# The backward pass of a gated S4 layer: two token tiles in turns at the opening of the last pass, a block of the gated gradient kept on chip, and a write on another queue

## The chip, the cores and the metric

The kernel runs on one core of a Trainium2 chip. The core has five engines, each with its own instruction stream: TensorE (PE in the profile, its weight loads PEld), VectorE (DVE), ScalarE (ACT), GpSimd (POOL) and SyncE (SP). DMAs are issued by SP, ACT and POOL. The metric is the device time of one execution in microseconds (us); the median over the runs is compared.

## The reference

The forward pass is a layer norm, an S4 convolution over the sequence, a SwiGLU feed-forward network whose output goes through a SiLU, and a gated sum. The program computes the output and the gradients of all inputs (B_x is not differentiated).

```python
x = A_u                                  # 1 x 2048 x 576
xn = _layernorm(x, axis=-1)
s = _A_ref(xn, A_re, A_im, B_re, B_im, C_re, C_im, log_dt, Dskip)
                                         # long convolution by FFT, 128 states
g = _silu(_B_ref(xn, w1, w3, w2))        # out = (silu(x w1) * (x w3)) w2, F = 4608
return x + s * g
...
_out, _vjp = jax.vjp(_f, A_u, A_A_re, ..., B_w1, B_w3, B_w2)
return (_out0, *_vjp(grad_out))
```

## The kernel before

Everything is in bf16 on the matmul side with f32 sums. The sequence of 2048 tokens is cut into 16 token tiles of 128 (LT), the width 576 (D) into two matmul pieces of 288, and the hidden width 4608 (F) into 36 blocks of 128 (FT) and 18 groups of 256. In the odd token tiles the 128 tokens stand in reversed order. The last pass takes the token tiles in the order 1, 3, .. 15, 0, 2, .. 14. "Tile i" of the last pass is the i-th of that order. Results of the odd ones go to a scratch array first (`odd`) and are written from there to the output with the tokens turned back.

The order of instructions on each engine is made by a scheduler from the program's order, from due times (`self.at`) and from `issue_after`, which puts an instruction behind another one. Buffers come from pools; a tile with the tag of another takes its slot, and a tile that takes a slot waits until the old one is read for the last time.

The stages, in the order in which they run:

1. Layer norm, convolution kernel and forward convolution beside the first half of the network (`ffn_hidden`).
2. `ffn_output`: for each of the 16 token tiles the product with w2 (`po`, L975), and then its epilogue. It works out `gs_t`, the gradient times the gate (L994), and stores it to `GS_dram` (L995) in four quarters of 144 columns.
3. `backward` opens. `ssm_bwd_conv` is a generator: `conv_bwd_quarter` for quarter 0 loads `gs` in four blocks of four token tiles (L1114), folds each (L1130, L1131), transforms it (`dft_folded`, L740), multiplies spectra on DVE (`Z`, L777 to L786, `ZZ`, L1161 and L1166) and transforms back (L751). Between its steps it yields to `phase6_group`, which for group 0 makes all its gradient tiles: `make(s)` is a product of the transposed gradient with w2 (`ph`, L1552), an ACT copy (L1555) and DVE products (L1568). The order written is: conv blocks 0 to 2, then `make` 0 to 2 and the last transposes, then conv block 3, then the rest.
4. The groups of the feed-forward backward, gi = 0 to 17. Each forms `gg_n` and `gu_n` (gradients of gate and up), stores them to `GG_dram` and `GU_dram` (L1573), and forms the weight gradients: `phase6_grad13` for w1 and w3 (L1610, L1620, L1622), and `phase6_grad2` for w2 (`pgw`, L1590). The w2 gradient of a group is made inside the same group, at its stages h1 and h3, except for groups 16 and 17: theirs come after the stores of group 17. From group 11 on, half steps of the S4 parameters are mixed in (`param_half`: PE L1224, DVE L1229 and L1232; loads `qT` and `gz` on SP, `pz` on ACT), and `phase5_blocks` turns their sums into the S4 gradients (POOL DMAs L1286, L1317, L1328). From there on all DMAs of SP keep the order in which they are written (`self.chain`).
5. The last pass, `phase6_inputs`. For each tile i there are 72 steps of two matmuls (L1657, 128 x 288): a block of `GG` or `GU` in transposed form (`acts`, loaded by a transposing DMA) against a row block of w1 or w3, also transposed (`wA`, `wT`). The 72 row blocks lie in pieces; `load_piece` loads one as five transposes into a slot that the groups have done with. Then come the layer norm's backward (`ln_bwd_tile`, L1668 to L1696, on DVE, ACT and POOL) and `ln_finish` (L1699), which writes the result (ACT queue, L1703) and at i = 5 and i = 9 one half of the reversed odd tiles (SP, L1706). There are two `acts` buffers, so that those of tile i + 2 can only be loaded when tile i has been multiplied. Parameter half steps stand at fixed steps of a tile (`stops`).

Where the last pass opens, SP's order is: `acts` of tile 0; ten transposes (`h_n` 1,22 and `h_n` 0,22); the GG half of tile 1; ten transposes (`gg_n` 0,29 and `gu_n` 1,29); the GU half of tile 1; `qT`, `gz`, `qT`, `gz`; `acts` of tile 2, and so on.

Of the kernel before, what the change touches and what calls it, by code (L numbers as in the profile page):

```python
# [14 lines left out]
BF16 = mybir.dt.bfloat16  # L15
I32 = mybir.dt.int32
I16 = mybir.dt.int16
P = 128
# [58 lines left out]
class K:  # L77
# [849 lines left out]
    def ffn_output(self, T0, TB):  # L927
# [9 lines left out]
        with self.pool(name="o_hc", bufs=1) as hpc, \  # L937
# [10 lines left out]
            self.epi = []  # L948
            w2 = []
# [29 lines left out]
            def finish(st):  # L979
# [16 lines left out]
                                  in_=gs_t[:].rearrange("p (g d) -> p g d", g=4))  # L996
                nc.vector.tensor_tensor(out=n4(g[:]), in0=p4(s_t[:]), in1=n4(g[:]), op=ALU.mult)
# [102 lines left out]
    def conv_bwd_quarter(self, g, kp, zp, ps, T0, TQ):  # L1100
# [9 lines left out]
        for b in range(NB if g == 0 else 1):  # L1110
            ts = slice(b * KT, (b + 1) * KT) if g == 0 else slice(0, LT)
            if g == 0:
                self.at(T0 - 170 + 40 * b if b < NB - 1 else T0)
            nc.sync.dma_start(out=gs[:, ts], in_=self.GS_dram[g, :, ts])  # L1114
# [9 lines left out]
        G = []  # L1124
        gm = kp.tile([P, NB, 2, W], BF16, name="gm")
        g4 = gs[:].rearrange("p (b k) w -> p b k w", k=KT)

        def fold(bs):
            lo, hi = g4[:, bs, 0:2], g4[:, bs, 3:1:-1]
            nc.vector.tensor_tensor(out=gm[:, bs], in0=lo, in1=hi, op=ALU.subtract)  # L1130
            nc.vector.tensor_tensor(out=lo, in0=lo, in1=hi, op=ALU.add)  # L1131
# [4 lines left out]
        for b in range(NB):  # L1136
            self.at(T0 + (TQ * 0.05 * b if g else 0))
            after = None
            if g == 0 and b == NB - 1:
                pt = ps.tile([P, 512], FP32, name="et_ps")  # L1140
                self.turn_go(LT - 1, pt[:].bitcast(BF16)[:, 0:cfg.DT * P].rearrange("p (c t) -> p c t", t=P), self.dft_last)
                yield
                self.at(T0)
                after = self.pe_last
            G.append(self.bgp.tile([P, 1, 2, KT, W], BF16, name=f"g_{b}"))
            if g == 0:
                fold(slice(b, b + 1))
            with self.tc.issue_after(after.ins) if after is not None else nullcontext():
                self.dft_folded(ps, self.cCS, (g4[:, b], gm[:, b]), G[b])
            if after is not None:  # L1150
                yield
# [192 lines left out]
    def backward(self, T0, TG, TQ, TC, TX, gctx, mats):  # L1344
# [12 lines left out]
        with ExitStack() as out:  # L1357
# [18 lines left out]
            conv = self.ssm_bwd_conv(T0, TQ, ps)  # L1376
            next(conv)
# [4 lines left out]
            group = self.phase6_group(0, cur, elp, gwp, ps_h, ps_gw)  # L1382
            next(group)
# [14 lines left out]
            for gi in range(NG):  # L1398
# [9 lines left out]
                for stage in group if gi == 0 else self.phase6_group(gi, cur, elp, gwp, ps_h, ps_gw):  # L1408
# [4 lines left out]
                    if stage in ("h1", "h3"):  # L1413
                        if gi < NG - 2:
                            w2(gi, stage == "h3")
                        if stage == "h3" and gi + 2 < NG:
                            self.phase6_load_h(gi + 2, T0 + TG * gi, inp)
                    if stage == "h1" and lastg:
                        self.load_piece(wT, inp, "gg_n", 0, 15, 7)
                        self.load_piece(wT, inp, "gu_n", 1, 15, 7)  # L1420
                        self.load_piece(wT, wp, "w2T", 1, 13, 2)
# [3 lines left out]
                    if stage == "stored":  # L1425
# [3 lines left out]
                        if lastg:  # L1429
# [3 lines left out]
                            for g in (NG - 2, NG - 1):  # L1433
                                for fl in range(2):
                                    w2(g, fl)
                                step()
                                self.phase5_step(self.half // 2)
                                self.phase5_step(self.half // 2)
                                if g == NG - 2:
                                    self.load_piece(wT, inp, "h_n", 1, 22, 7)  # L1440
                                else:
                                    self.load_piece(wT, inp, "h_n", 0, 22, 7)
                            acts.append(self.load_acts(1, (0,)))
# [11 lines left out]
            self.load_acts(1, (1,), acts[1])  # L1455
# [77 lines left out]
    def phase6_group(self, gi, tiles, elp, gwp, ps_h, ps_gw):  # L1533
# [24 lines left out]
        if gi == 0:  # L1558
            for s in range(3):
                make(s)  # L1560
            yield "early"
# [74 lines left out]
    def phase6_inputs(self, T2, TX, wT, acts, pool):  # L1636
# [6 lines left out]
        with pool(name="l_sb", bufs=2) as sb, pool(name="l_s1", bufs=1) as s1, \  # L1643
                pool(name="l_sm", bufs=4) as sm, pool(name="x_ps", bufs=2, space=bass.MemoryType.PSUM) as ps:
            for i in range(LT):
                self.at(T2 + TX * i)
                act, t = acts[i], self.order[i]
# [4 lines left out]
                go_t, o1 = go_o1[:, 0], go_o1[:, 1]  # L1652
                nc.scalar.dma_start(out=go_t, in_=self.tok("grad_out", t))
                stops = () if i in (0, LT - 1) else (14, 38, 62) if i in (2, 4, 6, 8) else (20, 50)
                for n, (ai, fi, w) in enumerate(steps):
                    for pi_, (po, pw) in enumerate(pieces):
                        self.pe_last = nc.tensor.matmul(px[pi_][:, 0:pw], lhsT=act[:, ai, fi, :], rhs=w[:, po:po + pw],  # L1657
                                                        start=(n == 0), stop=(n == len(steps) - 1))
                    if n == 8 and i > 0:
                        self.ln_finish()  # L1660
                    if i == LT - 1 and n in (20, 32, 44, 64):
                        self.phase5_step(self.half // 2)
                    if n in stops:
                        self.param_step()
                        self.phase5_step(self.half // 2)
                gx = s1.tile([P, D], FP32, name="gx7")
# [32 lines left out]
    def ln_finish(self):  # L1699
# [4 lines left out]
        if i in (5, 9):  # L1704
            q = slice(0, 4) if i == 5 else slice(4, 8)
            self.nc.sync.dma_start(out=self.turned(self.aps["out_1"].flatten_outer_dims(), q.start, q.stop), in_=self.odd["out_1"][q])  # L1706
# [99 lines left out]
```

## Time and profile before

| | |
|---|---|
| three runs, median | 1875.47 us (1872.55 to 1878.48) |
| the profiled execution, its own time | 1874.95 us |
| its span in the profile | 1873.2 us |
| mean granted TensorE clock over the span | 0.973 |
| PE busy | 1689.1 us, 90% of the span |
| PE weight loads busy | 1231.2 us, 66% |
| DVE busy | 1370.1 us, 73% |
| ACT busy | 910.0 us, 49% |
| POOL busy | 352.1 us, 19% |
| DMA | 417.27 MB, mean 223 GB/s |
| L1657, matmuls with wT | x1408, 182.5 us; 17.3 us idle before them, by wT |
| L1657, matmuls with wA | x896, 123.4 us; 19.6 us idle before them, 19.1 by acts |
| L1590 (w2 gradient) | x1152, 150.4 us |
| L1552 (gradient to the hidden width) | x1440, 173.0 us |

A busy engine is not one at its peak, and idle time counts only on the engine that ends last in that stage. So the page is read stage by stage: in a table of windows each line has its start and end, its length, then busy us (and number of instructions) of PE, PEld, DVE, ACT and POOL, PE's granted clock as a share of full speed, the busy share of the DMA engines, and GB/s. In a timeline each line has start, length, engine, line, operation, output and inputs, and in brackets the idle time before it and what ended it. "SPq" is SP's DMA queue: the length there is the time that SP was taken up with issuing.

### The profile page before, as it was taken

How to read it: one execution, taken by the hardware profiler on the slowest of the kernel's cores; microseconds unless marked ns; L12 is line 12 of the kernel's file. 1: busy time of each engine (PE TensorE's matmuls, PEld its weight loads, DVE VectorE, ACT ScalarE, POOL GpSimd, SP SyncE). 2: the span in 40 equal slices, each digit the busy share in tenths (PEclk: the TensorE clock that was granted, in tenths of full speed). 3: DMA queues.
4: the chain of work that ended last, by engine and by line, in shares of the span. 5: the costliest groups of instructions: out<-in, count | busy, mean ns of one | idle time of the engine just before them, and what ended most of it. 6: DMA issues, size and time to landing. Idle time of an engine off the chain costs nothing. (4 is left out here: it accounts for less than half of the span.)

```text
span 1873.2 us, 38325 instructions
## 1 busy us (share of the span) xinstructions
PE 1689.1 (90%) x15461; PEld 1231.2 (66%) x15516; DVE 1370.1 (73%) x2081; ACT 910.0 (49%) x1632; POOL 352.1 (19%) x567
## 2 busy tenths in 40 slices
PE   2999999999897999799999999999998968979997
PEld 0335555555353777578878887888777756868786
DVE  5538666768988555588694989759998954867675
ACT  3768888887563111465765756565444300001001
POOL 4021222222223111011111111111110242031032
PEclk9999999999998999899999999999999998989999
DMA  6579988887777997658666575579999899988993
GB/s 172 175 242 328 328 304 305 308 291 267 239 242 225 218 205 179 218 157 232 183 198 190 180 211 173 167 210 284 258 233 232 179 221 245 209 195 204 220 210 72
DMA packets 627231, 417.27 MB, mean 223 GB/s; under 512 B 424429, under 2 KB 567853, under 8 KB 622445
## 3 DMA queue, kind: packets, MB, share of 16 engines
q1 hardware_dynamic: 569820, 281.98, 58.3%
q0 software_dynamic: 30672, 106.50, 16.8%
q10 hardware_dynamic: 26560, 26.35, 4.7%
q8 instruction: 121, 1.98, 0.4%
q14 instruction: 58, 0.47, 0.1%
HBM read 135.74 MB, written 190.89 MB: 174 GB/s over the span
## 5 line engine op out<-in xcount | busy, mean ns | idle before, releaser
L1657 PEld LDWEIGHTS <-acts 128*128 128x128 bf16 x2304 | 228.4, 100 | 100.7 <-DMA acts<-GG_dram 19.8
L1610 PEld LDWEIGHTS <-xn_bf 128*128 128x128 bf16 x2304 | 225.6, 98 | 37.0 <-issue 10.1
L1229 DVE TENSOR_TENSOR pr_q<-et_ps,pz 128x1024 f32<-128x1024 f32 x144 | 176.0, 1222 | 48.9 <-PE et_ps L1224 41.8
L1657 PE MATMUL px<-wT,acts 128*128 128x288 bf16 x1408 | 182.5, 289 | 17.3 <-DMA wT<-in_B_w_dram 17.3
L901 PEld LDWEIGHTS <-xnT 128*128 128x128 bf16 x1152 | 107.4, 98 | 115.5 <-issue 25.3
L1232 DVE TENSOR_REDUCE S_all<-pr_q 128x32 f32<-128x1024 f32 x144 | 175.3, 1217 | 3.4
L1552 PE MATMUL ph<-w2T,goT 128*128 128x256 bf16 x1440 | 173.0, 275 | 1.6 <-ACT gh L1555 1.4
L901 PE MATMUL pg<-wmB_w,xnT 128*128 128x512 bf16 x526 | 147.9, 382 | 16.4 <-DVE g_t L915 9.5
L901 PE MATMUL pu<-wmB_w,xnT 128*128 128x512 bf16 x571 | 155.4, 379 | 0.4
L1590 PE MATMUL pgw<-go_o,h_n 128*128 128x288 bf16 x1152 | 150.4, 287 | 4.1 <-DVE h_n L1530 2.8
L1552 PEld LDWEIGHTS <-goT 128*128 128x128 bf16 x1440 | 140.4, 99 | 19.7 <-issue 2.8
L1610 PE MATMUL pgw<-gu_n,xn_bf 128*128 128x256 bf16 x1152 | 135.6, 276 | 7.0 <-ACT gw L1594 6.8
L1657 PE MATMUL px<-wA,acts 128*128 128x288 bf16 x896 | 123.4, 298 | 19.6 <-DMA acts<-GG_dram 19.1
L1590 PEld LDWEIGHTS <-h_n 128*128 128x128 bf16 x1152 | 112.6, 98 | 32.5 <-DVE h_n L1530 3.3
L1610 PE MATMUL pgw<-gg_n,xn_bf 128*128 128x256 bf16 x1152 | 130.2, 273 | 1.6 <-ACT gw L1612 1.6
L913 ACT ACTIVATE s_t<-pg 128x512 bf16<-128x512 f32 x144 | 87.8, 610 | 89.4 <-PE pu L909 44.7
L1685 ACT ACTIVATE go<-gx 128x576 bf16<-128x576 f32 x16 | 10.9, 683 | 220.7 <-DVE gx L1668 220.7
L1555 ACT CAST gh<-ph 128x512 bf16<-128x512 f32 x144 | 82.0, 600 | 71.6 <-PE ph L1552 54.0
L590 ACT ACTIVATE cs_k<-et_ps 128x512 bf16<-128x512 int16 x216 | 112.1, 643 | 1.7 <-PE et_ps L589 1.3
L1612 ACT CAST gw<-pgw 128x256 bf16<-128x256 f32 x144 | 53.9, 375 | 99.3 <-PE pgw L1610 96.7
L924 POOL DMA_DIRECT2D G_dram<-g_t x72 | 52.3, 727 | 232.3 <-DVE g_t L915 223.9
L918 ACT CAST u_t<-pu 128x512 bf16<-128x512 f32 x144 | 86.9, 604 | 12.0 <-PE pu L901 12.0
(302 smaller groups left out, 3232.2 us busy)
## 6 DMA issues: line engine op xcount, KB each, us to landing
U_dram<-u_t POOLq DMA_DIRECT2D x72, 256.0 KB, 4.3
G_dram<-g_t POOLq DMA_DIRECT2D x72, 256.0 KB, 4.0
H_dram<-h_t SPq DMA_DIRECT2D x72, 256.0 KB, 4.7
Q_dram<-q_k SPq DMA_DIRECT2D x36, 512.0 KB, 4.2
h_n<-U_dram POOLq DMA_DIRECT2D x18, 1024.0 KB, 8.7
gg_n<-G_dram POOLq DMA_DIRECT2D x18, 1024.0 KB, 5.9
GU_dram<-gu_n SPq DMA_DIRECT2D x36, 512.0 KB, 3.6
GG_dram<-gg_n SPq DMA_DIRECT2D x36, 512.0 KB, 8.3
```

The costliest lines, as they stand in the source:

```text
L590: nc.scalar.activation(out=CS[:, :, o:o + 256], in_=pt[:].bitcast(I16)[:, :, 0::2], func=ACT.Sin, scale=6.283184 / 2 ** 16)
L901: ins = nc.tensor.matmul(pt[:], lhsT=xnT[:, c, ts], rhs=wm[w][:, c, :], start=(q == 0 and c == 0), stop=(q == 1 and c == nfull - 1))
L913: nc.scalar.activation(out=s_t[:, :, q, :], in_=pgv, func=ACT.Silu)
L918: nc.scalar.copy(out=u_t[:, :, q, :], in_=pu[:].rearrange("p (g f) -> p g f", g=ng))
L1229: nc.vector.tensor_tensor(out=pr[:].rearrange("p r k e -> p r (k e)"), in0=T[h][:].rearrange("p k z d a -> p (k z d a)")[:, None].to_broad ...
L1232: nc.vector.tensor_reduce(out=self.S_all[:, :, d0:d0 + 4], in_=pr[:].rearrange("p r k (d a) -> p (r k) d a", d=4), op=ALU.add, axis=AX.X)
L1552: self.pe_last = nc.tensor.matmul(ph[j][:, k, :].rearrange("p (a f) -> p a f", f=P), lhsT=lw, rhs=rh, start=(n == 0), stop=(n == nfull))
L1555: self.sc(lambda: nc.scalar.copy(out=gh[:, j], in_=ph[j][:]))
L1590: self.pe_last = nc.tensor.matmul(pgw[pi_][:, 0:pw], lhsT=hn[:, tt, fl * P:(fl + 1) * P], rhs=go_o[:, tt, po:po + pw], start=(tt == 0), st ...
L1610: self.pe_last = nc.tensor.matmul(pw_[:, 0:FG], lhsT=self.xn_bf[:, tt, c * P:(c + 1) * P], rhs=nat[:, tt, :], start=(tt == 0), stop=(tt == ...
L1612: self.sc(lambda: nc.scalar.copy(out=gw[:, c], in_=pw_[:, 0:FG]))
L1657: self.pe_last = nc.tensor.matmul(px[pi_][:, 0:pw], lhsT=act[:, ai, fi, :], rhs=w[:, po:po + pw], start=(n == 0), stop=(n == len(steps) - 1))
```

## The change

Four parts:

1. `ffn_output` copies the first 144 columns of `gs_t` of the last four token tiles into a tile on chip, `gs_end`. The last block of quarter 0 of the backward convolution is taken from there, and its load from `GS_dram` is gone. `backward` now starts `phase6_group` first, with `make(0)` alone; the four blocks of the convolution stand behind its last matmul; then `make(1)` and `make(2)`.
2. The w2 gradient of group 16 is made inside group 16, like that of the groups before it. In its stage out_11 the piece `h_n` (1,22) is loaded. After the stores of group 17 only group 17's w2 gradient is left. `ready` is the number of row blocks whose pieces are loaded by then, 51.
3. SP's order where the last pass opens: `acts` of tile 0, `acts` of tile 1, the fifteen transposes of the last three pieces, `qT`, `gz`, `qT`, `gz`, `acts` of tile 2. Tiles 0 and 1 are multiplied in turns: steps 0 to 50 of tile 0, then of tile 1, 51 to 57 of each, 58 to 71 of each. There are no parameter half steps in them; tile 2 has four (three before), tile 3 has three (two before).
4. The reversed odd tiles of the second output are written at i = 10 and i = 13 of `ln_finish`, from the POOL queue.

```diff
--- before.py
+++ after.py
@@ -946,6 +946,7 @@
             gap.tile([P, 1024], BF16, name="o_gap")
             self.hc_loads = []
             self.epi = []
+            self.gs_end = self.matp.tile([P, cfg.KT, D // 4], BF16, name="gs_end", tag="skip_row")
             w2 = []
             F0 = LT
             w2a = self.ktp.tile([P, F0, D], BF16, name="w2a", tag="KT")
@@ -994,6 +995,8 @@
                 nc.vector.tensor_tensor(out=p4(gs_t[:]), in0=n4(go_t[:]), in1=n4(g[:]), op=ALU.mult)
                 nc.sync.dma_start(out=self.GS_dram[:, :, i, :].rearrange("g p d -> p g d"),
                                   in_=gs_t[:].rearrange("p (g d) -> p g d", g=4))
+                if i >= LT - cfg.KT:
+                    nc.scalar.copy(out=self.gs_end[:, i - LT + cfg.KT], in_=gs_t[:, 0:D // 4])
                 nc.vector.tensor_tensor(out=n4(g[:]), in0=p4(s_t[:]), in1=n4(g[:]), op=ALU.mult)
                 o0 = ip.tile([P, D], BF16, name="o0")
                 self.epi.append(nc.vector.tensor_tensor(out=o0[:], in0=g[:], in1=x_t[:], op=ALU.add))
@@ -1107,10 +1110,10 @@
         fl = lambda t_: t_[:].rearrange("p q r k d -> p (q r) (k d)")
         self.at(T0)
         gs = kp.tile([P, LT, W], BF16, name="gs")
-        for b in range(NB if g == 0 else 1):
+        for b in range(NB - 1 if g == 0 else 1):
             ts = slice(b * KT, (b + 1) * KT) if g == 0 else slice(0, LT)
             if g == 0:
-                self.at(T0 - 170 + 40 * b if b < NB - 1 else T0)
+                self.at(T0 - 170 + 40 * b)
             nc.sync.dma_start(out=gs[:, ts], in_=self.GS_dram[g, :, ts])
         self.at(T0 if g else T0 - 100)
         for b in range(NB):
@@ -1122,11 +1125,18 @@
             with self.tc.issue_after(self.epi[2 * b + 7].ins) if g == 0 else nullcontext():
                 self.spectrum_variants(A2[b], Az[b])
         G = []
+        first = self.pe_last
         gm = kp.tile([P, NB, 2, W], BF16, name="gm")
         g4 = gs[:].rearrange("p (b k) w -> p b k w", k=KT)
 
+        sums = [g4[:, b] for b in range(NB)]
+        if g == 0:
+            sums[NB - 1] = self.gs_end
+
         def fold(bs):
             lo, hi = g4[:, bs, 0:2], g4[:, bs, 3:1:-1]
+            if g == 0 and bs.stop == NB:
+                lo, hi = self.gs_end[:, None, 0:2], self.gs_end[:, None, 3:1:-1]
             nc.vector.tensor_tensor(out=gm[:, bs], in0=lo, in1=hi, op=ALU.subtract)
             nc.vector.tensor_tensor(out=lo, in0=lo, in1=hi, op=ALU.add)
 
@@ -1145,9 +1155,11 @@
             G.append(self.bgp.tile([P, 1, 2, KT, W], BF16, name=f"g_{b}"))
             if g == 0:
                 fold(slice(b, b + 1))
+            if g == 0 and b == 0:
+                after = first
             with self.tc.issue_after(after.ins) if after is not None else nullcontext():
-                self.dft_folded(ps, self.cCS, (g4[:, b], gm[:, b]), G[b])
-            if after is not None:
+                self.dft_folded(ps, self.cCS, (sums[b], gm[:, b]), G[b])
+            if g == 0 and b == NB - 1:
                 yield
         st = self.bgp.tile([P, 2, D // 64, 2, 8, LT], BF16, name="gk_st")
         nxt = None
@@ -1373,13 +1385,15 @@
             self.hn = {}
             self.w2Ts = {}
             self.tail = None
-            conv = self.ssm_bwd_conv(T0, TQ, ps)
-            next(conv)
             for g in range(2):
                 self.phase6_load_h(g, T0 - TG, inp)
             cur = self.phase6_load(0, T0 - TG, TG, wp, inp)
             self.at(T0)
             group = self.phase6_group(0, cur, elp, gwp, ps_h, ps_gw)
+            next(group)
+            conv = self.ssm_bwd_conv(T0, TQ, ps)
+            next(conv)
+            self.at(T0)
             next(group)
             next(conv)
             for _ in cur[-1]:
@@ -1411,10 +1425,12 @@
                     if stage in ("h2", "h3", "out_11_0", "out_11_1", "out_11_2", "out_11_3", "out_10_0", "out_10_1"):
                         next(prep, None)
                     if stage in ("h1", "h3"):
-                        if gi < NG - 2:
+                        if gi < NG - 1:
                             w2(gi, stage == "h3")
                         if stage == "h3" and gi + 2 < NG:
                             self.phase6_load_h(gi + 2, T0 + TG * gi, inp)
+                    if stage == "out_11" and gi == NG - 2:
+                        self.load_piece(wT, inp, "h_n", 1, 22, 7)
                     if stage == "h1" and lastg:
                         self.load_piece(wT, inp, "gg_n", 0, 15, 7)
                         self.load_piece(wT, inp, "gu_n", 1, 15, 7)
@@ -1430,17 +1446,14 @@
                             self.hold = []
                             self.phase5_open(elp)
                             acts = [self.load_acts(0)]
-                            for g in (NG - 2, NG - 1):
-                                for fl in range(2):
-                                    w2(g, fl)
+                            for fl in range(2):
+                                w2(gi, fl)
                                 step()
                                 self.phase5_step(self.half // 2)
                                 self.phase5_step(self.half // 2)
-                                if g == NG - 2:
-                                    self.load_piece(wT, inp, "h_n", 1, 22, 7)
-                                else:
-                                    self.load_piece(wT, inp, "h_n", 0, 22, 7)
-                            acts.append(self.load_acts(1, (0,)))
+                            acts.append(self.load_acts(1))
+                            self.ready = sum(part[2] for part in wT)
+                            self.load_piece(wT, inp, "h_n", 0, 22, 7)
                     elif stage in ("h1", "h3", "out_11", "out_10", "end") and gi >= GP and not (lastg and stage in ("out_10", "end")):
                         step()
                         if lastg and stage == "out_11":
@@ -1452,7 +1465,6 @@
                 self.phase5_step(self.half // 2)
             self.load_piece(wT, inp, "gg_n", 0, 29, 7)
             self.load_piece(wT, inp, "gu_n", 1, 29, 7)
-            self.load_acts(1, (1,), acts[1])
             self.param_flush()
             ffn.close()
             self.phase6_inputs(T2, TX, wT, acts, pool)
@@ -1556,7 +1568,9 @@
             made[s] = gh
 
         if gi == 0:
-            for s in range(3):
+            make(0)
+            yield "open"
+            for s in range(1, 3):
                 make(s)
             yield "early"
         for s in range(LH // 2):
@@ -1642,27 +1656,44 @@
         self.ln_rest = []
         with pool(name="l_sb", bufs=2) as sb, pool(name="l_s1", bufs=1) as s1, \
                 pool(name="l_sm", bufs=4) as sm, pool(name="x_ps", bufs=2, space=bass.MemoryType.PSUM) as ps:
-            for i in range(LT):
-                self.at(T2 + TX * i)
-                act, t = acts[i], self.order[i]
+            def begin(i):
+                t = self.order[i]
                 px = [ps.tile([P, 512], FP32, name=f"px{pi_}") for pi_ in range(len(pieces))]
                 gxs = sb.tile([P, D], FP32, name="gxs7")
                 nc.scalar.dma_start(out=gxs[:], in_=self.GXN_dram[:, t, :])
                 go_o1 = self.rowp.tile([P, 2, D], BF16, name="go7", tag=f"w2r{i % 2}")
-                go_t, o1 = go_o1[:, 0], go_o1[:, 1]
-                nc.scalar.dma_start(out=go_t, in_=self.tok("grad_out", t))
-                stops = () if i in (0, LT - 1) else (14, 38, 62) if i in (2, 4, 6, 8) else (20, 50)
-                for n, (ai, fi, w) in enumerate(steps):
+                nc.scalar.dma_start(out=go_o1[:, 0], in_=self.tok("grad_out", t))
+                return px, gxs, go_o1[:, 0], go_o1[:, 1]
+
+            def product(i, px, n0, n1, stops):
+                for n in range(n0, n1):
+                    ai, fi, w = steps[n]
                     for pi_, (po, pw) in enumerate(pieces):
-                        self.pe_last = nc.tensor.matmul(px[pi_][:, 0:pw], lhsT=act[:, ai, fi, :], rhs=w[:, po:po + pw],
+                        self.pe_last = nc.tensor.matmul(px[pi_][:, 0:pw], lhsT=acts[i][:, ai, fi, :], rhs=w[:, po:po + pw],
                                                         start=(n == 0), stop=(n == len(steps) - 1))
-                    if n == 8 and i > 0:
+                    if n == 8 and i > 1:
                         self.ln_finish()
                     if i == LT - 1 and n in (20, 32, 44, 64):
                         self.phase5_step(self.half // 2)
                     if n in stops:
                         self.param_step()
                         self.phase5_step(self.half // 2)
+
+            n1, n2, n3 = self.ready, self.ready + 7, len(steps)
+            self.at(T2)
+            opened = [begin(0), begin(1)]
+            for n0, n in ((0, n1), (n1, n2), (n2, n3)):
+                for i in range(2):
+                    product(i, opened[i][0], n0, n, ())
+            for i in range(LT):
+                self.at(T2 + TX * i)
+                t = self.order[i]
+                px, gxs, go_t, o1 = opened[i] if i < 2 else begin(i)
+                if i == 1:
+                    self.ln_finish()
+                stops = () if i in (0, 1, LT - 1) else (12, 28, 44, 62) if i == 2 else (14, 38, 62) if i in (3, 4, 6, 8) else (20, 50)
+                if i > 1:
+                    product(i, px, 0, n3, stops)
                 gx = s1.tile([P, D], FP32, name="gx7")
                 for pi_, (po, pw) in enumerate(pieces):
                     nc.vector.tensor_tensor(out=gx[:, po:po + pw].rearrange("p (g d) -> p g d", g=4),
@@ -1701,9 +1732,9 @@
         self.nc.vector.scalar_tensor_tensor(out=o1, in0=gx[:], scalar=self.rstd[:, t:t + 1], in1=gs[:],
                                             op0=ALU.mult, op1=ALU.add)
         self.nc.scalar.dma_start(out=self.tok("out_1", t), in_=o1)
-        if i in (5, 9):
-            q = slice(0, 4) if i == 5 else slice(4, 8)
-            self.nc.sync.dma_start(out=self.turned(self.aps["out_1"].flatten_outer_dims(), q.start, q.stop), in_=self.odd["out_1"][q])
+        if i in (10, 13):
+            q = slice(0, 4) if i == 10 else slice(4, 8)
+            self.nc.gpsimd.dma_start(out=self.turned(self.aps["out_1"].flatten_outer_dims(), q.start, q.stop), in_=self.odd["out_1"][q])
 
 
 from concourse._compat import with_exitstack
```

## The prediction

> **What bounds the kernel now.** I read four views in this order: the page's chain of work that ended last, a table of windows, the timelines of TensorE (PE) and of the sync engine's DMA queue (SPq) in the stages that the change touches, and VectorE's (DVE) timeline where PE waited for it. The chain first:
>
> ```profile
> PE 12%; DMA 2%; SPq 2%; DVE 1%; issue 1%; POOL 0%; ACT 0%; DVEq 0%; ACTq 0%; POOLq 0%
> ```
>
> It ends in L1657 (the last pass) and steps over SPq's transposes, so in the last pass the transfers that feed the product end last. The windows give start:end, length, then busy us per engine, granted clock, DMA share:
>
> ```profile
> 757.00:814.00 57.00, 38.94 (x329) 31.92 (x328) 36.44 (x80) 34.12 (x58) 2.68 (x5) 0.85 0.51 165
> 1404.00:1512.60 108.60, 98.83 (x935) 82.79 (x933) 100.72 (x115) 44.79 (x78) 21.78 (x39) 0.97 0.90 212
> 1512.60:1556.00 43.40, 21.28 (x143) 14.49 (x140) 13.10 (x36) 1.92 (x5) 18.45 (x35) 0.79 1.08 205
> 1556.00:1873.00 317.00, 291.06 (x2442) 231.49 (x2442) 212.04 (x277) 30.27 (x58) 64.81 (x119) 0.95 0.86 194
> ```
>
> PE is idle for 18.0 us in the first window (the backward pass opens), 22.1 in the third (the last pass opens, with the DMA engines full), 26 in the fourth. The second is nearly full on DVE: work put there must fit PE's 9.8 us of slack. In the opening and the middle of the last pass PE's timeline names what it waited for:
>
> ```profile
> 1517.98 3.45 PE L1657 MATMUL px<-wA,acts 128*128 128x288 bf16 x15 [4.95 <-DMA acts<-GG_dram]
> ...
> 1544.15 0.40 PE L1657 MATMUL px<-wT,acts 128*128 128x288 bf16 x1 [8.07 <-DMA wT<-in_B_w_dram]
> ...
> 1554.25 0.40 PE L1657 MATMUL px<-wT,acts 128*128 128x288 bf16 x1 [5.30 <-DMA wT<-in_B_w_dram]
> ...
> 1665.98 6.36 PE L1657 MATMUL px<-wA,acts 128*128 128x288 bf16 x30 [10.52 <-DMA acts<-GG_dram]
> ...
> 1747.28 6.66 PE L1657 MATMUL px<-wA,acts 128*128 128x288 bf16 x30 [3.60 <-DMA acts<-GG_dram]
> ```
>
> SPq's timeline shows why tile 6 was late: a queue that elsewhere issues without a gap stands still before its `qT` and `gz`, and the `acts` of tile 6 stand behind them:
>
> ```profile
> 1633.86 0.70 SPq L1706 DMA_DIRECT2D out_dram<-odd_out  x1
> 1644.34 2.44 SPq L1489 DMA_TRANSPOSE qT<-Q_dram  x1
> 1652.58 1.88 SPq L1214 DMA_DIRECT2D gz<-gK_dram  x2
> 1655.90 5.99 SPq L1489 DMA_TRANSPOSE acts<-GG_dram  x1
> ```
>
> In the program SP and ACT share eight DMA semaphores in turn: a DMA waits for the one issued eight earlier. There `qT` waits for ACT's `pz`, and `gz` for `odd_out` of tile 4, whose scale stands on POOL behind eight DMAs of L1317. Before tile 10 the order is alike. DVE's timeline where the backward pass opens:
>
> ```profile
> 766.50 0.74 DVE L987 SCALAR_TENSOR_TENSOR e<-po,g 128x576 f32<-128x576 f32 x1
> 782.98 0.31 DVE L1130 TENSOR_TENSOR gm<-gs 128x288 bf16<-128x288 bf16 x1 [11.60 <-DMA gs<-GS_dram]
> 786.44 0.76 DVE L777 TENSOR_TENSOR Z<-a,g 128x1152 bf16<-128x1152 bf16 x1 [2.81 <-ACT g L742]
> ```
>
> The last quarter of `gs` goes out and comes back before it can be folded; then DVE runs without a gap to 813.8, where group 0's first gate product starts on PE.
>
> **The change, part by part.** The profiled execution took 1874.95 us, its span is 1873.2 (1.75 lie around it); the median of the three runs is 1875.47, 0.52 above. Gains below are in the span and are taken from the median.
>
> *The block kept on chip, and the first gradient block made ahead.* Added: four ACT copies of 128x144; ACT is busy 34 of 57 us there, so they are hidden, and at the 0.3 us of a DVE fold of like size they would cost 1.2 without that cover. Removed: one SP load of 144 KB, 10.9 us from its issue at 772.1 to the fold. The fold can follow `gs_t` (768.9) plus a copy. But PE's order now has L1552 first, and its second tile uses a PSUM bank that L987 reads until 767.24: PE does five matmuls from 761.2 and stands 5.3 us, against 3.53 for `cCSb` now. From 767.24 the other 27 matmuls of L1552 take 3.7 (row of 26), the four blocks of L740 (eight rows of two matmuls each, a row every 0.125 us at full speed, every 0.24 behind a wait) 4.0 to 7.7; with the casts, `g` of block 3 is ready between 778.5 and 782.5. I take the later, as the clock is then low: the `Z` chain starts 3.9 earlier than 786.44. In DVE's new order eight operations of that chain (six with a step of 0.67, two of 0.37, 4.8 us) go behind group 0's `h_n`, though only 3.0 for its first one: 4.0 taken. Put off: 1.4 us of L751 on PE. Gain 3.9 + 4.0 - 1.4 = 6.5. Bounds: 1 (`Z` starts no earlier, and the longer PE wait of 1.8 counts) to 11 (8 earlier).
>
> *The w2 gradient of group 16 made in its own group.* No matmul is added or taken away. 64 matmuls of L1590 (7.9 us) go from behind the last stores to between group 16's gradient blocks, where they fit the slack of 9.8. But 27 more stand on PE before the step that frees SP's last `qT`: SP's 15 transposes, the last stores and the `acts` of tile 0 come 27 x 0.1225 = 3.3 later, so tile 0 starts near 1521.2 (bounds 1518 to 1523). Of the old cover after the last stores, nothing else waits.
>
> *Two tiles in turns behind fewer transposes.* Five pieces move ahead, into an SP gap of group 16. Behind `acts` of tiles 0 and 1 come 15 transposes (20.5 us, from 13.65 for ten), then `qT`, `gz` twice (8.2, from 1557.7 to 1565.9). `acts` of tile 1 are issued by 1533, the transposes by 1553.5, `gz` by 1561.7. PE ends both tiles near 1562, against 1579.2 now. But each tile's `acts` hold one of two buffers to the end, and tile 2's stand behind `gz`: issued 1561.7, landed some 8 us later (7.0 to 10.0 elsewhere) at 1570. PE waits about 8 us, and tile 2 starts 9.2 earlier than now. Taken off: two parameter half steps moved to tiles 2 and 3, 2 x 0.44 on PE = 0.9 (tile 2 has four, 4 x 4.88 = 19.5 us on DVE beside a tile of 18.7; 0.6 for that); the slow clock behind the wait, where thirty matmuls took 6.36, against 30 x 0.1225 = 3.68: 2.7. Gain 9.2 - 0.9 - 0.6 - 2.7 = 5.0. Bounds: -1 (DVE is late by a whole half step more, 4.9, and 1 of landing) to 9.
>
> The Trainium skill (TensorE: Matmul & The Clock Gate, part 1) says that an idle window of about 3.4 us halves PE's clock until a busy one of the same length has passed. By that rule a wait costs 1.7 us of slowness, and this part would gain 6.0.
>
> *The reversed write on POOL.* Two DMAs of 576 KB leave SP (0.70 each to issue) and the turn of eight; POOL issues them for about 0.53 each (rows of L1317). In POOL's new order the first stands behind tile 3's `gxs`, not at tile 10, and waits there for `odd_out` of tile 3; the second behind tile 7's. Queued behind the first are eight DMAs of L1317 and tile 4's scale, which has a tile (18 us) to spare against a landing of 4 us. What counts is the turn of eight: before tile 6, SP's `acts` now wait only for a `qT` and PE, and the ACT transfers ahead are those of tiles 3 and 5. The stall of 10.52 and its slow clock of 2.7 go: 13.2. Before tile 10 `gz` still waits for `odd_out` of tile 6 and `acts` for a `gxs` of ACT, so I count its stall (3.60 + 0.52, and 3.0 of slow clock: 7.1) as unchanged. Bounds: 0 (it comes back elsewhere) to 20.3.
>
> Sum: 6.5 + 5.0 + 13.2 = 24.7; 1875.47 - 24.7 = 1850.8 us.
>
> **The rivals.**
>
> *The middle runs smooth*: the second stall goes too. For: no wait on a same tile's ACT work is left. Against: a DMA share of 0.86. 1850.8 - 7.1 = 1843.7.
>
> *The stall in the middle comes back at another tile*: for it, SP's queue is 15 of 18.6 us full per tile; against, the order of waits. 1850.8 + 13.2 = 1864.0. The Trainium skill (DMA: Bandwidth & Descriptors, Issuing engines are not separate DMA queues) says that issuing from another engine saves only the issue time, as all run on the same 16 DMA engines; by that the move to POOL is worth its 1.4 us of issue and this rival holds. The trace speaks for a wait of the queue, not of the engines: 10 us without an issue.
>
> *The edit at the backward opening does not do what it says*: L1552 waits for the epilogue's bank, and DVE gains nothing. 1850.8 + 6.5 = 1857.3.
>
> *Slower: tiles 2 to 7 become bound by SP's transposes.* Tiles 0 and 1 end together, so `acts` of 2 and 3 are issued together with the parameter loads and PE has no lead. If the pair goes on at the opening's pace (7.35 + 6.96 = 14.3, then 8.5 to land: 22.8 against 18.5), each of six tiles waits 4.3 and pays 2.7 of clock: 42 us, that is 42 - 24.7 = 17.3 slower: 1893. It decides from 4.1 us per tile. For: the DMA engines are full at that point. Against: from 1566 on a pair takes 10.8.
>
> **How the numbers follow.** Chances: forecast 0.37, smooth 0.22, stall elsewhere 0.20, backward opening without effect 0.09, slower 0.12. The time is that of the forecast. About 0.3% (5.6 us) is what a measurement of this kernel can tell from no change. Faster by more: the first three and the fourth but for the ends of their bounds, 0.88 less 0.11 = 0.77; of that 0.11, 0.09 goes within, with 0.02 of the slower case: 0.11; slower 0.12. Range: from 1838 (smooth, with 6 more of the first two parts' bounds) to 1872 (the returned stall with 8 less of them); outside lie the slower case and some of the tails.
>
> **What would show it.** In the changed profile: PE stands about 5 us near 762 before L1552 and the fold of block 3 no longer waits for `GS_dram`; group 0's first gate product starts near 806. Tile 0 starts near 1521, tile 2 near 1570 behind a wait of 6 to 9 us for `acts`. No gap of SPq over 5 us between 1600 and 1660, and no wait of PE over 2 us for tile 6. Wrong: waits for `acts` at several tiles from 2 to 8, or for `et_ps` in tile 2; the first gate product later than 812; tile 2 after 1577.

## The result and the profile after

The changed kernel took 1859.82 us in the median (1858.30 to 1860.98, four runs) against 1876.97 (1872.55 to 1878.92, four runs). The ratio is 0.9911, with an interval of 0.9891 to 0.9932: 17 us faster, where 24.7 were forecast. Its profiled execution took 1858.30 us with a span of 1856.5, which is 16.7 less than the span before. The ratios below leave out executions more than 1.5% above the fastest of the same kernel (two of e4, one of e7, two of the kernel before), while the medians do not.

First the chain that ended last, on the page of the changed kernel. The queue of SP now has 5% of it (2% before):

```profile
PE 12%; SPq 5%; DMA 3%; DVE 2%; POOL 1%; issue 1%; ACT 0%; ACTq 0%; DVEq 0%; POOLq 0%
```

The table of windows of the changed kernel, with stages that answer to the four shown before: start:end, length, busy us of PE, PEld, DVE, ACT and POOL, granted clock, DMA share, GB/s.

```profile
755.00:812.00 57.00, 42.03 (x363) 33.53 (x362) 39.47 (x83) 34.04 (x59) 3.75 (x7) 0.88 0.62 194
1400.00:1510.00 110.00, 98.29 (x952) 84.34 (x951) 99.26 (x112) 46.94 (x80) 19.27 (x35) 0.98 0.98 217
1510.00:1551.00 41.00, 34.72 (x280) 26.64 (x275) 17.94 (x42) 2.02 (x5) 18.76 (x36) 0.98 1.10 221
1551.00:1856.00 305.00, 272.74 (x2315) 217.80 (x2313) 211.87 (x277) 30.15 (x58) 70.31 (x125) 0.96 1.00 197
```

Where the last pass opens, PE now works 34.7 of 41 us (21.3 of 43.4 before): its waits for `wT` are nearly gone. In the rest of the pass it still idles 32 us in 305. PE's timeline of the changed kernel says for what (its first line is from the opening of the backward pass):

```profile
766.22 5.71 PE L1564 MATMUL ph<-w2T,goT 128*128 128x256 bf16 x30 [6.82 <-DMA w2T<-w2r]
...
1547.53 0.28 PE L1672 MATMUL px<-wT,acts 128*128 128x288 bf16 x1 [3.37 <-DMA wT<-in_B_w_dram]
...
1563.57 6.29 PE L1672 MATMUL px<-wA,acts 128*128 128x288 bf16 x26 [8.13 <-DMA acts<-GG_dram]
...
1716.83 1.01 PE L1236 MATMUL et_ps<-gz,qT 128*128 128x128 bf16 x8 [7.42 <-DMA gz<-gK_dram]
```

The wait of 8.13 is that of tile 2 for its `acts`, as forecast. The waits of 10.52 and 3.60 before tiles 6 and 10 are gone, both of them. In their place stands one of 7.42 in tile 9, and it is for `gz`, an operand of the parameter steps. On SP's queue, in the same execution, one sees the `qT` ahead of it take 8.76 us to issue, where the five before it in the pass took 2.6 to 3.2:

```profile
1700.38 8.76 SPq L1501 DMA_TRANSPOSE qT<-Q_dram  x1
1709.19 1.22 SPq L1226 DMA_DIRECT2D gz<-gK_dram  x2
1710.52 5.70 SPq L1501 DMA_TRANSPOSE qT<-Q_dram  x1
1716.26 1.23 SPq L1226 DMA_DIRECT2D gz<-gK_dram  x2
```

POOL issues the second write of the reversed odd tiles at 1698.5, two microseconds ahead of that `qT`. This is where the experiments begin.

### The profile page after: what moved, and what is told of

Same layout as the page of the kernel before. It is cut to its first block, busy times and chain, and to the rows that moved or that the text cites. A ratio compares the mean times of both kernels' runs of the same rounds, so it can differ in the third digit from the quotient of the medians.

```text
span 1856.5 us, 38320 instructions
## 1 busy us (share of the span) xinstructions
PE 1679.0 (90%) x15461; PEld 1228.5 (66%) x15516; DVE 1370.5 (74%) x2081; ACT 909.5 (49%) x1636; POOL 354.7 (19%) x569
## 3 DMA queue, kind: packets, MB, share of 16 engines
q0 software_dynamic: 31728, 107.69, 17.2%
## 5 line engine op out<-in xcount | busy, mean ns | idle before, releaser
L1624 PEld LDWEIGHTS <-xn_bf 128*128 128x128 bf16 x2304 | 224.7, 98 | 34.8 <-issue 8.7
L1624 PE MATMUL pgw<-gu_n,xn_bf 128*128 128x256 bf16 x1152 | 133.9, 274 | 6.5 <-ACT gw L1608 6.3
L1624 PE MATMUL pgw<-gg_n,xn_bf 128*128 128x256 bf16 x1152 | 130.0, 273 | 0.6 <-ACT gw L1626 0.6
L1609 POOL DMA_DIRECT2D out_dram<-gw x36 | 20.0, 555 | 387.1 <-ACT gw L1608 334.1
```

The source lines that it names most:

```text
L1624: self.pe_last = nc.tensor.matmul(pw_[:, 0:FG], lhsT=self.xn_bf[:, tt, c * P:(c + 1) * P], rhs=nat[:, tt, :], start=(tt == 0), stop=(tt == ...
```

## The experiments

To compare runs by stage I read six marks from each profile: the last matmul of `po`, the first gate product (L1610, in the changed kernel L1624), SP's issue of `acts` of tile 0 and of tile 2, DVE's second read of `px` (L1668, L1699) for tiles 3 and 15. The stretches between them in us:

| kernel | po to gate product | gate product to acts 0 | acts 0 to acts 2 | acts 2 to end of tile 3 | tile 3 to tile 15 |
|---|---|---|---|---|---|
| before | 52.9 | 690.5 | 61.6 | 51.2 | 245.4 |
| after | 46.1 | 696.7 | 52.6 | 53.2 | 238.0 |
| after, no write (e1) | 46.7 | 697.2 | 52.4 | 53.0 | 228.8 |
| after, writes on SP (e2) | 46.5 | 694.9 | 52.1 | 52.5 | 245.1 |
| before, no write (e3) | 50.5 | 692.3 | 60.9 | 51.0 | 226.9 |
| before, writes on POOL (e4) | 54.7 | 692.6 | 59.8 | 50.5 | 248.1 |
| after, writes late (e5) | 45.5 | 703.1 | 52.4 | 52.8 | 228.4 |
| after, one write (e6) | 47.2 | 696.9 | 54.6 | 52.7 | 239.5 |
| before, backward opening (e7) | 46.4 | 693.1 | 62.7 | 51.0 | 244.9 |
| before, last pass opening (e8) | 53.3 | 699.0 | 52.8 | 53.1 | 245.4 |
| after, one write last (e9) | 46.3 | 706.9 | 52.4 | 52.6 | 228.8 |
| before, one write last (e10) | 54.5 | 696.1 | 62.4 | 51.1 | 233.0 |
| before, block on chip (e11) | 52.4 | 695.3 | 61.2 | 51.0 | 246.1 |
| before, gradient first (e12) | 48.4 | 705.4 | 61.6 | 51.0 | 247.1 |

The second column moves by 15 us between kernels in which the second part of the change is absent (690.5 to 705.4) and by 12 between those that have it (694.9 to 706.9). The first repeats within some 4 us, the others within 1 to 3 where the kernels are alike, and tell more than a total does. The kernel before ran again beside each group of experiments, with medians of 1872.98 us (e1 to e4), 1881.43 (e5 to e8) and 1878.72 (e9 to e12); each ratio is to the one beside it.

### The reversed writes: which queue, or the write itself (e1 to e4)

My theory was Q: a DMA of SP waits for the one issued eight earlier, SP and ACT share that turn, and the write on SP brings the stalls by shifting it. The wait for `gz` in tile 9 suggested a rival, W: the write itself holds up what is behind it. Four kernels were made to tell them apart: each of the two kernels without the write, and each with the other's placement. Without it (e1, e3) the odd tiles of the second output are left unwritten.

```diff
 # e1: these lines of ln_finish left out (e3: its lines for i in (5, 9), on nc.sync)
-        if i in (10, 13):
-            q = ...
-            self.nc.gpsimd.dma_start(out=self.turned(...), in_=self.odd["out_1"][q])
 # e2: the changed kernel with the old lines
+        if i in (5, 9):
+            q = slice(0, 4) if i == 5 else slice(4, 8)
+            self.nc.sync.dma_start(...)
 # e4: the kernel before with the new lines (i in (10, 13), gpsimd)
```

> The changed kernel without the two writes of the reversed odd tiles (the odd tiles of the second output are not written). Theory W, the write itself: 576 KB from DRAM to DRAM hold the DMA engines for 10 to 14 us, and SP's transposes and gz behind it come late, whatever queue issues it. Then the wait of 7.42 us for gz in tile 9 goes, tile 9 loses 11 us less, and the time is 1848 to 1851. Theory Q, the turn of eight that SP and ACT share: the write on POOL is outside it, so the wait for gz stays and the time is 1857 to 1861.

Measured: 1853.08 us, ratio to the kernel before 0.9855 (0.9797 to 0.9913). The wait of 7.42 for `gz` is gone, as W had it; tile 3 to tile 15 in 228.8 us, 9.2 less than in the changed kernel. The time lies between the two forecasts.

> The changed kernel with the writes back on SP at i = 5 and 9. Theory Q: SP's qT and gz before the acts of tiles 6 and 10 wait for ACT again, and both stalls come back: 1870 to 1875. Theory W: the write only falls at another moment: 1855 to 1863.

Measured: 1865.85 us, ratio 0.9976 (0.9935 to 1.0017). The stalls are back at tiles 6 and 10, of 10.59 and 3.35 us; tile 3 to tile 15 in 245.1, as before the change. Here Q was right on the places, and the time again lies between the forecasts. SP's waits in this kernel, between 1600 and 1650 us, name what held the queue ahead of tile 6 (us in total, times, longest):

```profile
SPq L1501 <- DMA pz<-PZ_dram: 11.6, 1, 11.6
SPq L1226 <- DMA odd_out<-go: 8.7, 1, 8.7
```

Both are DMAs of ACT, by the turn of eight. The write itself moves from 1619.5 to 1625.9; the `pz` for which SP waits is issued only after that, at 1627.04, and has landed at 1629.66.

> The kernel before without the two writes (the odd tiles of the second output are not written). Theory W: the stalls of 10.52 and 3.60 us at tiles 6 and 10 go with their slow clock, 20 us: 1854 to 1858. Theory Q: the turn of eight shifts by one and by two, and SP still waits for ACT in the middle of the pass: less than 10 us gained.

Measured: 1854.78 us, ratio 0.9872 (0.9819 to 0.9925). Tile 3 to tile 15 in 226.9, 18.5 less than with the write. That is W's number; Q had less than 10. But without the write its place in the turn is gone as well: SP's next `qT` waits 1.2 us there instead of 9.7. So this run alone does not separate the two.

> The kernel before with the fourth part of the change alone. My prediction's term: 13.2 us gained, 1862, with the stall at tile 6 gone and that at tile 10 kept. Theory W: the stalls go from tiles 6 and 10 to where POOL issues the writes; the gain is 5 to 13 us.

Measured: 1878.98 us, ratio 0.9998 (0.9961 to 1.0035). Nothing is gained, less than either forecast. PE's timeline of this kernel shows the stalls of tiles 6 and 10 replaced by two waits for `gz`, in tiles 5 and 9 (and one of 3.17 for `acts` in tile 8):

```profile
1650.27 1.01 PE L1224 MATMUL et_ps<-gz,qT 128*128 128x128 bf16 x8 [6.04 <-DMA gz<-gK_dram]
...
1738.32 1.01 PE L1224 MATMUL et_ps<-gz,qT 128*128 128x128 bf16 x8 [4.80 <-DMA gz<-gK_dram]
```

So the write costs 16 to 19 us in this pass on SP and, on POOL, 9 us in the changed kernel and 21 in the kernel before. On POOL it is outside the shared turn, and the kernels compared (e1, e3) have the same turn without it: there the write itself is the cause, as W says. On SP the waits that the profile shows are Q's.

How the write moves is seen where it runs. In the kernel before that is from 1635.4 to 1643.1. A window ahead of it and one in it (columns as above; the last two are the DMA share and GB/s):

```profile
1626.00:1633.00 7.00, 6.60 (x59) 5.27 (x57) 6.70 (x10) 0.84 (x2) 0.00 (x0) 1.00 1.21 262
1636.00:1643.00 7.00, 7.00 (x64) 5.67 (x63) 6.82 (x11) 0.78 (x2) 1.12 (x3) 1.00 0.36 118
```

And the line of SP's queue (q1) for the second window, of the same kernel: packets, MB, share of 16 engines.

```profile
q1 hardware_dynamic: 501, 0.57, 23.8%
```

On this queue nothing but the write moves there: 0.57 MB in packets of 1152 bytes, and 23.8% of 16 engines is 3.8 engines (most of the rest of the 118 GB/s is ACT's `pz`). The write has the shape 4 x 128 x 576, and it runs on four engines. The `qT` behind it is issued at 1644.34, just after the write ends, but not because of its end: SP waits 9.7 us for a `pz` of ACT, issued at 1638.54 and landed at 1644.28. Its `gz` then waits 5.7 us for the `odd_out` of tile 4, landed at 1652.51, nine microseconds after the write. SP had issued no transpose that the write could hold up. At most it delayed that `pz`, which took 5.7 us to land (3.3 to 7.9 in e3).

In the changed kernel it is on POOL's queue (q0), beside SP's transposes. A window ahead of it and one in it:

```profile
1695.00:1700.00 5.00, 5.00 (x44) 3.99 (x42) 4.74 (x5) 0.00 (x0) 1.17 (x1) 1.00 1.22 276
1704.00:1709.00 5.00, 4.08 (x34) 3.04 (x32) 4.08 (x7) 0.78 (x2) 0.53 (x2) 1.00 1.23 123
```

The queues' lines of the second window:

```profile
q1 hardware_dynamic: 580, 0.15, 98.9%
q0 software_dynamic: 96, 0.44, 22.9%
```

The write again takes 22.9% of 16 engines, 3.7. SP's queue looks busy (98.9%) and moves 0.15 MB in 5 us. In the five microseconds of the first window its line is:

```profile
q1 hardware_dynamic: 4854, 1.23, 112.7%
```

That is eight times as much. In the packets of the trace, 206 of the 574 of 256 bytes on SP's queue take 180 ns or more beside the write, and these make up 88% of their time; in the first window 18 is usual. A DMA share of 1.22 and 1.23 in the two windows tells nothing of this; the GB/s do.

The Trainium skill (DMA: Bandwidth & Descriptors, Why a DMA increments its semaphore by 16 and not by 1) says that a DMA runs on the largest number of engines up to 16 that divides the slowest dimension of both its sides. For four token tiles that is four, and the trace agrees with 3.8 and 3.7.

### The write late, and as one (e5, e6, e9, e10)

```diff
 # e5: two writes on POOL, behind the gxs of tile 13
+        self.gxs_last = eng.tensor_tensor(out=gs[:], in0=gs[:], in1=go_t, op=ALU.add)
...
+                if i == 13:
+                    for q in (slice(0, 4), slice(4, 8)):
+                        with self.tc.issue_after(self.gxs_last.ins):
+                            nc.gpsimd.dma_start(out=self.turned(...), in_=self.odd["out_1"][q])
 # e6: in ln_finish, in place of the two, one write of eight token tiles on POOL
+        if i == 10:
+            self.nc.gpsimd.dma_start(out=self.turned(...), in_=self.odd["out_1"][:])
 # e9 (changed kernel) and e10 (kernel before): in place of the two, one write on SP behind the acts of the last tile
+                if i + 2 == LT - 1:
+                    self.sp(lambda: nc.sync.dma_start(out=self.turned(...), in_=self.odd["out_1"][:]))
```

The diff of the change said i = 10 and 13, but the scheduler put the POOL writes behind the `gxs` of tiles 3 and 7, as soon as their data could be there. `issue_after` on an instruction of POOL itself is what holds the one of e5 back.

> The changed kernel with both writes on POOL behind the gxs of tile 13, where SP has no transposes left. Theory W, now sharper (in the traces the write moves some 95 KB per us, as four of the sixteen engines would, and for its 6 to 8 us the transposes get almost nothing): nothing is left to be held up, so the time is that of the changed kernel without the writes, 7 to 10 us under the changed kernel. Rival: the two writes end after the last tile and set the end; then it is as long as the changed kernel or longer.

Measured: 1860.86 us, ratio 0.9877 (0.9813 to 0.9940). Tile 3 to tile 15 in 228.4, as without the writes. But from there to the end are 15.7 us, 10.6 to 10.8 in all other runs: both theories were right, one on the pass and one on the tail.

> The changed kernel with one write of all eight odd tiles (1152 KB) on POOL behind the gxs of tile 7. Theory W with engines by the outermost count: eight rows of tiles give eight engines, so the write takes as long as one of four tiles (6 to 8 us) and holds up SP once and not twice: 2 to 5 us under the changed kernel. Rival, bytes alone: twice the bytes hold up SP twice as long in one place, 5 us over the changed kernel or more.

Measured: 1856.56 us, ratio 0.9839 (0.9767 to 0.9910). Tile 3 to tile 15 in 239.5, 1.5 over the changed kernel: neither number. A wait of 3.61 for `acts` and one of 1.38 for `gz` fall where the write runs. The write of eight stops the transposes as that of four does, once (the `qT` beside it takes 9.15 us to issue); the saving of the second write is not to be seen in this one profile, whereas the total came out lower. This run settles nothing on the time.

> The changed kernel with one write of all eight odd tiles on SP, behind the acts of the last tile. Theory W: no transpose is left to be held up and POOL's tail stays free, so the last pass is as without the writes (tile 3 to tile 15 in some 230 us, 239 in the changed kernel) and the end is not moved: 9 us under the changed kernel. Rival: the write comes too late and moves the end by 3 us or more.

Measured: 1858.90 us, ratio 0.9867 (0.9830 to 0.9905). Tile 3 to tile 15 in 228.8, and 10.6 to the end: the pass of the kernel without the writes. By the ratios it is 8 us under the changed kernel, where 9 were expected, but the intervals overlap. SP's queue in a window of its write, four microseconds long:

```profile
q1 hardware_dynamic: 608, 0.70, 48.9%
```

48.9% of 16 engines is 7.8: the write of 8 x 128 x 576 runs on eight, as the Trainium skill's rule above has it, and moves twice as much per microsecond.

> The kernel before with that one write behind the acts of the last tile and nothing else of the change. Theory W: as without the writes, tile 3 to tile 15 in some 227 us for 245, so 16 to 20 us gained, about as much as the whole change gained. Rival (the stalls come from the turn of eight that SP and ACT share): less than 8 us.

Measured: 1858.47 us, ratio 0.9874 (0.9832 to 0.9917). Tile 3 to tile 15 in 233.0, 12.4 less than before, where 16 to 20 were expected: 6 us more than in e3, most of it in tiles 11 and 13, with waits of 2.03 for `acts` and 2.59 for DVE's `pr_q`. The timed gain is larger than 12.4. This one edit to the kernel before gains as much as the whole change did. The version with both, e9, has the best pass, but its total cannot be told from that of e10: the second column of its profiled execution was the longest of all (706.9).

### The two openings alone (e7, e8, e11, e12)

```diff
 # e7: of the change, gs_end, sums, fold, make(0) first, conv behind it
 # e8: of the change, w2 gradient of group 16, SP's order, begin/product in turns, stops
 # e11: gs_end and its fold alone, order as before
-                self.dft_folded(ps, self.cCS, (g4[:, b], gm[:, b]), G[b])
+                self.dft_folded(ps, self.cCS, (sums[b], gm[:, b]), G[b])
 # e12: make(0) first and conv behind it alone, the last block of gs loaded from DRAM
```

> The kernel before with the first part of the change alone (block kept on chip, first gradient block made ahead). My prediction: 6.5 us gained, nothing lost later. Rival (the opening does not do what it says): within 2 us.

Measured: 1873.66 us, ratio 0.9949 (0.9915 to 0.9982). The opening takes 46.4 us against 52.9. By the interval 3 to 16 us are gained, so the rival of under 2 is out.

> The kernel before with the second and third part alone (w2 gradient of group 16 in its group, two tiles in turns). My prediction: 5.0 us gained, with a wait of some 8 us for the acts of tile 2 and the stalls at tiles 6 and 10 as before. Rival: SP's transposes bound tiles 2 to 7, and it is slower than before.

Measured: 1874.66 us, ratio 0.9953 (0.9917 to 0.9989). PE's timeline has the forecast wait for tile 2 (first line), and that for tile 6 as before (second):

```profile
1576.39 4.02 PE L1656 MATMUL px<-wA,acts 128*128 128x288 bf16 x16 [8.21 <-DMA acts<-GG_dram]
...
1668.69 3.54 PE L1656 MATMUL px<-wA,acts 128*128 128x288 bf16 x14 [9.97 <-DMA acts<-GG_dram]
```

> The kernel before with the block kept on chip alone, in the old order. If the gain of the backward opening is the load that is gone, the first gate product starts 5 us or more earlier against the start of that stage. If it is the new order, under 2 us.

Measured: 1877.71 us, ratio 0.9993 (0.9966 to 1.0021). The opening takes 52.4 us. The gain of the load alone is hidden: ahead of `Z`, DVE now stands for the fold of the next quarter, whose `gs` comes from DRAM as well:

```profile
784.46 0.76 DVE L1139 TENSOR_TENSOR gm<-gs 128x1152 bf16<-128x1152 bf16 x1 [12.63 <-DMA gs<-GS_dram]
```

> The kernel before with the first gradient block made ahead alone; the last block is still loaded from DRAM. If the gain is the load, the first gate product starts within 2 us of before, or later by the longer wait; if it is the order, 5 us or more earlier.

Measured: 1886.13 us, ratio 1.0001 (0.9968 to 1.0033). The opening takes 48.4 us, so in this one profile most of the gain is the order. The profiled execution lost it again in the groups (705.4 to `acts` of tile 0), in the column that moves by as much between like kernels. The total does not show the gain: the executions scatter from 1868.69 to 1890.81, and their median is 7 us above that of the kernel before.

## Why the prediction was right or wrong

**The backward opening: right, by a path that differed in parts.** Forecast 6.5 us. The median of the five kernels with none of it is 53.3 and of the seven with all of it 46.4: 6.9. The `Z` chain starts 3.1 us earlier against the last `po` matmul (3.9 forecast). DVE's timeline of the changed kernel shows the fold without its load, and the wait that is left, for the casts:

```profile
768.86 0.29 DVE L1140 TENSOR_TENSOR gm<-gs_end 128x288 bf16<-128x288 bf16 x1
...
781.50 0.76 DVE L777 TENSOR_TENSOR Z<-a,g 128x1152 bf16<-128x1152 bf16 x1 [11.92 <-ACT g L742]
```

The step "PE does five matmuls from 761.2 and stands 5.3 us" did not occur: thirty matmuls start together behind a wait of 6.82, which the profile puts down to `w2T`. The first gate product starts at 805.2 (806 forecast). The 3.9 stood for the load that is gone and the 4.0 for DVE's new order; alone, in one profile each, the order gives 4.9 and the load 0.9 (kernels alike in this stretch differ by up to 4).

**The last pass's opening: right in its mechanism, too large by about 2 us.** Forecast 5.0. Medians of the kernels without and with it, column by column: `acts` of tile 0 come 4.1 later (693.1 to 697.2; 3.3 forecast); from there to `acts` of tile 2 it takes 9.2 less (61.6 to 52.4; 7.5 forecast); from there to the end of tile 3 it takes 1.8 more (51.0 to 52.8). That makes 3.3; its first term is a median of the column that spreads by 12 to 15, so it is uncertain by some us. The wait of 8.13 for tile 2, and the fit of its start (1570 less 6.5 forecast, 1563.57 measured), hold; tile 0 starts at 1511.76, 3 us ahead of its forecast less 6.5. The timed run of this part alone gave 2 to 16 us, so the 3.3 rests on the stages. The rival that SP's transposes would bound tiles 2 to 7 is out: no wait of PE over 2.4 us falls between tiles 2 and 8 of the changed kernel. Another sign failed: SP's queue does have gaps of 5.6 us at 1619 and 9.0 at 1656, where none over 5 was forecast, but PE does not wait for them. Such gaps were there before too (3.8 us at 1613, 4.3 at 1702), so "elsewhere issues without a gap" was misread.

**The reversed write: the step that failed.** "What counts is the turn of eight" was the ground for 13.2 us. Of the old stalls it was true: with the write back on SP they return, and SP waits in them for ACT's DMAs (e2). What the sum left at nothing is the write itself on its new queue. It takes four engines, for 6 to 13 us each time, and the second one nearly stops SP's transposes while it runs: tile 9 waits 7.42 for `gz`, and the pass is 9.2 longer than without the writes (238.0 against 228.8 in e1). So tile 3 to tile 15 went from 245.4 to 238.0, 7.4, and in the kernel before the same edit gave nothing (248.1, with 226.9 in e3). Both old stalls went, where I had one go and one stay, and one came in tile 9 that I had not listed. The rival beside it, a stall at another tile, had the right place for the error, and its 1864.0 is nearer to the 1859.82 measured than the forecast is. I set it aside on "a wait of the queue, not of the engines: 10 us without an issue". That was a right reading of the write on SP; it says nothing of what the same write does from POOL, beside transposes that are no longer held. The GB/s of the same microseconds (118, with a DMA share of 0.36) would have shown that the write runs on few engines. The Trainium skill (DMA: Bandwidth & Descriptors, Issuing engines are not separate DMA queues) has all queues on the same 16 engines, and e4 agrees: the move to POOL was worth nothing there.

**The sum.** 6.9 + 3.3 + 7.4 is 17.6, for 17.2 measured between the medians. That they fit so closely is in part luck: the first two are medians over many kernels, and the columns of the two profiles alone give 6.8 - 6.2 + 9.0 - 2.0 + 7.4 = 15.0. The mis-sized terms were the write (5.8 too much) and the opening (2 too much). The range held the time, and the sign followed from the first two parts alone.

## What to carry to other kernels

For a queue that stands still beside a large DMA, two things are to be read: SP's waits, which say for what it stands (here by the turn of eight, for ACT's DMAs), and the GB/s of that window. A DMA share of 4/16, or one near 1 with an eighth of the bytes, said here that the transfer ran on few engines. A change of queue mends the first and not the second. Put such a transfer where nothing waits behind it, here behind the last transposes (e10: one edit for 0.9874), and look in the instruction order whether a "later" in the source is later on its queue. Where totals move by 10 us between executions, compare the stage that was edited, over all runs that share it.

## What was not expected of the hardware

- A DRAM to DRAM write of 4 x 128 rows of 1152 bytes moves some 80 GB/s (0.57 MB in 7 us) on 3.8 engines; of 8 x 128 rows, some 175 GB/s (0.70 MB in 4 us) on 7.8.
- Beside it, when it comes from POOL, SP's transposes fall from 1.23 MB in 5 us to 0.15 MB; of their 574 packets of 256 bytes 206 take 180 ns or more, instead of 18.
- The time from the first gate product to the first `acts` differs by 12 to 15 us between profiled executions of kernels alike in it. In the two longest (e9, e12) PE waits 14.7 and 12.8 us for `gz` there, against 4.6 in the kernel before; why `gz` comes late stays open.
